# A planner entry for the expert products: a negative extra latency, priorities as before

## The chip, the cores and the metric

The kernel runs on one core of a Trainium2 chip. The metric is the device time of one execution in microseconds; of three runs shown for the kernel before the change the median is 987.2 us (985.83 to 988.81).

## What is computed

Three layers in one program: attention with rotary embedding, a dense feed-forward layer with a rational activation, and a mixture of experts with one expert per token. The change lies in the third.

```python
def _moe2_ref(x, w_gate, w1, w2):          # x: 2304 tokens x 512, 8 experts, hidden 1024
    logits = x @ w_gate
    expert_idx = np.argmax(logits, axis=1)
    ...
    for e in range(E):
        mask = expert_idx == e
        xe = x[mask]
        h = np.maximum(xe @ w1[e], 0.0)
        ye = h @ w2[e]
        out[mask] = gate_w[mask, None] * ye
```

## The kernel before

**The experts' tiles.** Tokens are sorted by expert into tiles t of at most 128 tokens. Every product is made of float32 values split into a high part (a rounded copy, made by ScalarE) and a low part (the value less its high part, made by VectorE or GpSimd), so one product is three matmuls: high by high, low by high, high by low. A tile has these steps, each an entry of a list with the name that the texts here use:

- `gx.t` (GpSimd, L925): an indirect DMA gathers the tile's rows. From t=10 on it takes its row numbers from a column that two small DMAs of SyncE bring in first, `cl.t` (L971).
- `xT.t` (TensorE, L1025): four transposes; `xH.et`, `xL.et` (ScalarE L1030, VectorE L1031): high and low part.
- `sA.t.c` (ScalarE, L1008) and `sL.t.c` (L1011; VectorE, but GpSimd for c=3 and c=7 and two others): high and low part of the weight piece c of the tile's expert, 128 by 1024. Pieces 0 to 3 belong to the first product, 4 to 7 to the second. A ring of five buffers holds the split pieces; `wl.t.c` (SyncE, L941) loads a raw piece once the low part of the tile before has been made from its buffer.
- `e1.t.k` (TensorE, L1044), k=0 to 3: the first product, six matmuls of 512 columns each, by weight piece k. Its last two read the low part `sL.t.k`.
- `rl.t` (ScalarE, L1050): the ReLU; `hT.t.0`, `hT.t.1` (TensorE, L1054): eight transposes; `hH.t.j`, `hL.t.j` (ScalarE L1060, VectorE L1061).
- `e2.t.k` (TensorE, L1071), k=0 to 3: the second product by weight piece 4+k, six matmuls; the third and the sixth read the low part.
- `fn.t` (L1077, L1078): scaling; `fs.t` (GpSimd, L1080): an indirect DMA scatters the rows to the output.

In the steady state TensorE does `e1` of tile t and then `e2` of tile t-1. While the first tiles run, VectorE also works through the second half of the routing, `B.c0` to `B.re` (L819 to L882), which places the remaining tokens; small copies for it run on ScalarE (L822, L824, L834, L844, L853, L854).

**What sets the order.** Nothing of this is written in the order in which it runs. `record` (L1113) and `step` (L1085) hand each step to `Plan.add` with an urgency, an engine, an assumed length `t`, what it reads and writes, and an extra latency `lat`. `Plan.order` (L85) then simulates five engines at build time: each takes, of the steps that are ready about now, the one with the lowest urgency. The instructions are emitted in that order, so it fixes the order on every engine. A step's result counts as ready at its end plus `AFTER` of its engine (0.3 us on TensorE) plus `lat`, and 0.1 us less for a step on the same engine:

```python
AFTER=dict(P=.3,V=.17,A=.17,G=.12,D=2.1)
...
x=end if ops[j][4]!=ops[i][4] or ops[i][4]=='D' else end-.1
if x>ready[j]: ready[j]=x
...
clock[e]=t+o[5]; end=t+o[5]+s.AFTER[e]+o[11]
```

Both products accumulate into one buffer (`eh`, `epsO`), so each `e1.t.k` depends on `e1.t.k-1`, and in this simulation it could start 0.2 us after that one's end at the earliest. The assumed times are used for the order alone; on the chip each instruction waits only for the semaphores of what it reads and writes.

Tiles 0 to 17 go through this list (`MIN`=18). What follows is emitted in a fixed order of code: `run` (L1134) and, here for the two last half tiles, `both` (L989).

Of the kernel before, what the change touches and what calls it, by code (L numbers as in the profile page):

```python
# [15 lines left out]
P=128  # L16
# [443 lines left out]
def phase1b(tc, plan, xT, w, ab, wg, x2, part, lg, ident, cp, xo3, keep, pre=()):  # L460
# [5 lines left out]
    if 1:  # L466
# [192 lines left out]
        for F in range(NS):  # L659
            s,k=steps[F]; h,g=ST[s]; t=TS(F); e=1 if last(F) else 0  # L660
            op(t+.1,f'm1.{F}',mm1,F)
            op(t+.8,f'au.{F}',a_u,F); op(t+.81,f'ae.{F}',a_e,F); op(t+.82,f'w1.{F}',a_w,F,0); op(t+.83,f'w2.{F}',a_w,F,1)
            op(t+2.2,f'p0.{F}',a_p,F,0); op(t+2.7,f'p1.{F}',a_p,F,1)
            t=TS(F+1)
            for d,n,fn,*a in ((.5,'ln',a_r,0),(.51,'ex',a_r,1),(.52,'q0',a_m,0),(.53,'q1',a_m,1),(1.5,'q2',a_m,2),(2.0,'gH',a_gH),(2.01,'gL',a_gL)): op(t+d,f'{n}.{F}',fn,F,*a)
            op(TS(F+LAG)+(0 if last(F) else .2),f'm2.{F}',mm2,F)
            if last(F):
                te=TS(F+LAG)
                for i in range(NTC): op(te+.4+.01*i,f'ev.{s}.{i}',o_ev,s,i); op(te+.405+.01*i,f'wr.{s}.{i}',o_wr,s,i)
                for i in range(NTC):  # L670
                    c=g*NTC+i
                    if h==0: continue
                    for d,x,n,fn in ((1,3.7,'tr',o_tr),(2,0,'sb',o_sb),(2,.1,'sl',o_sl)):
                        op(TS(F+LAG+d+i)+x if g<3 else TS(F+LAG+1)+1.4*i+.3*d+x/9 if g==3 else TS(F+LAG)+2+1.2*i+.3*d+x/9 if g==4 else te+.5+.9*i+.4*d+x/9,f'{n}.{c}',fn,c)
                if h:
                    for d,x,n,fn in ((NTC+1,3.7,'lg',o_lg),(NTC+2,0,'lc',o_lc),(NTC+2,3.7,'lt',o_lt),(NTC+3,0,'fi',o_fin)):
                        op(TS(F+LAG+d)+x if g<3 else TS(F+LAG+d-2)+x if g==3 else TS(F+LAG+d-3)+x if g==4 else te+3.2+.4*(d-NTC-1)+x/9,f'{n}.{g}',fn,g)
            if h==1 and k==len(FS[s])-4:
                t=max([t for n,t in rank.items() if n[:2]=='wr']+[TS(F)+3.5])
                for i in range(NTC): op(t+.01+.01*i,f'ld.{g*NTC+i}',o_ld,g*NTC+i)  # L680
# [214 lines left out]
class Experts:  # L895
# [147 lines left out]
            for hf in range(2):  # L1043
                s.T.matmul(h[hf],lhsT=d[z][:,k],rhs=w[wz][:,hf*512:hf*512+512],start=(k==0 and n==0),stop=(k==3 and n==2))  # L1044
    def mm1(s,t,k):
        s.op(f'e1.{t}.{k}',s.mm1_,t,k,eng='P',t=1.38,r=[(('eX',t%2),z) for z in 'HL']+[(('ew',t,k),z) for z in 'HL'],w=[(('eh',),0)],
            after=[f'{n}.{s.NS-1-i}' for n in ('ae','au','p0','p1') for i in range(2)] if t==k==0 else [])
    def relu_(s,t):
        d=s.D[t]; d['hr']=s.once(('hr',t%2),lambda: s.tag(6+t%2,1,2,512))
# [20 lines left out]
            for n,(z,wz) in enumerate((('hH',0),('hL',0),('hH',1))):  # L1070
                s.T.matmul(o,lhsT=d[z,j][:,kk],rhs=w[wz][:,i*512:i*512+512],start=(f==0 and n==0),stop=(f==7 and n==2))  # L1071
    def mm2(s,t,k):
        s.op(f'e2.{t}.{k}',s.mm2_,t,k,eng='P',t=1.38,r=[(('ehs',k//2,t%2),z) for z in 'HL']+[(('ew',t,4+k),z) for z in 'HL'],w=[(('epsO',),0)],after=['ev.11.2'] if t==k==0 else [])
    def fin_(s,t,z):
        g,i=s.rt.at(s.rt.gate,t); x,ix=s.rt.at(s.rt.sidx,t); o=s.once('o',lambda: s.tag(14,0,2,512))[:,t%2]
        if z==0:
            if t<4: s.A.activation(o,s.got['psO'],AF.Copy,scale=g[:,i:i+1])  # L1077
            else: s.V.tensor_scalar(o,s.got['psO'],g[:,i:i+1],None,ALU.mult)  # L1078
            return
        s.D.pop(t); s.nc.gpsimd.indirect_dma_start(out=s.out,out_offset=bass.IndirectOffsetOnAxis(ap=x[:,ix:ix+1],axis=0),in_=o,in_offset=None,bounds_check=NT-1,oob_is_err=False)  # L1080
# [100 lines left out]
```

## Time and profile before

| what | value |
|---|---|
| median of three runs | 987.2 us |
| the profiled execution's own time | 987.96 us |
| its span, first to last instruction | 986.2 us |
| TensorE busy | 946.6 us (96%) |
| VectorE, ScalarE, GpSimd busy | 826.9, 794.2, 746.5 us |
| mean granted TensorE clock | 0.993 |

The profiled execution is 0.8 us above the median, and 1.8 us of its time lie around its span. Its span has the attention first, the dense layer to about 738 us, an interleaved stretch in which the experts' first tiles and the routing run, and the experts alone from about 784 us on. PE is TensorE's matmuls, PEld its weight loads, DVE is VectorE, ACT ScalarE, POOL GpSimd, SPq the queue of SyncE, which issues DMAs. Matmuls are pipelined, so one of 512 columns is shown with some 0.4 us where its successor starts 0.23 us later.

### The profile page before, as it was taken

How to read it: one execution, taken by the hardware profiler on the slowest of the kernel's cores; microseconds unless marked ns; L12 is line 12 of the kernel's file. 1: busy time of each engine (PE TensorE's matmuls, PEld its weight loads, DVE VectorE, ACT ScalarE, POOL GpSimd, SP SyncE). 2: the span in 40 equal slices, each digit the busy share in tenths (PEclk: the TensorE clock that was granted, in tenths of full speed). 3: DMA queues.
4: the chain of work that ended last, by engine and by line, in shares of the span. 5: the costliest groups of instructions: out<-in, count | busy, mean ns of one | idle time of the engine just before them, and what ended most of it. 6: DMA issues, size and time to landing. Idle time of an engine off the chain costs nothing.

```text
span 986.2 us, 17395 instructions
## 1 busy us (share of the span) xinstructions
PE 946.6 (96%) x5402; PEld 834.4 (85%) x5402; DVE 826.9 (84%) x1451; ACT 794.2 (81%) x1538; POOL 746.5 (76%) x678
## 2 busy tenths in 40 slices
PE   5899999999988999999999999999999999999997
PEld 3889999999986898999999899898877788888873
DVE  6888999999999889999988676768998877777772
ACT  4899999999997888887777676766678788888881
POOL 3999999999448999998988576665574776767752
PEclk9999999999999999999999999999999999999999
DMA  7889797988724443432403021211611211561143
GB/s 241 236 226 220 208 226 209 228 209 194 207 84 153 142 137 121 137 122 78 146 2 96 11 87 28 80 40 34 231 53 49 49 40 54 180 227 44 44 123 106
DMA packets 55594, 125.81 MB, mean 128 GB/s; under 512 B 10947, under 2 KB 17219, under 8 KB 55492
## 3 DMA queue, kind: packets, MB, share of 16 engines
q1 hardware_dynamic: 52372, 114.65, 41.1%
q0 software_dynamic: 3120, 9.96, 3.2%
q8 instruction: 45, 0.74, 0.3%
q14 instruction: 57, 0.47, 0.2%
HBM read 146.63 MB, written 19.18 MB: 168 GB/s over the span
## 4 chain that ended last, share of the span: by engine, by line
PE 66%; ACT 12%; POOL 6%; DMA 6%; DVE 6%; issue 4%; SPq 0%; POOLq 0%; ACTq 0%; DVEq 0%
PE h L517 18%; PE acc L525 18%; PE h L1044 10%; PE acc L1071 9%; DMA st<-h 4%; ACT p L219 3%; ACT pTH L266 3%; PE sc L199 2%; PE ps L258 2%; PE av L280 2%; PE acc L1054 2%; ACT h L179 1%; POOL h L181 1%; ACT tm L286 1%; PE m L580 1%
## 5 line engine op out<-in xcount | busy, mean ns | idle before, releaser
L517 PE MATMUL h<-xH,w 128*128 128x384 f32 x768 | 214.3, 341 | 4.2 <-ACT gH L548 2.3
L525 PE MATMUL acc<-w,gH 128*128 128x512 f32 x576 | 150.0, 396 | 2.8 <-ACT gH L548 2.7
L517 PEld LDWEIGHTS h<-xH,w 128*128 128x128 f32 x768 | 140.9, 188 | 9.0 <-ACT gH L548 2.5
L517 PE MATMUL h<-xL,w 128*128 128x384 f32 x384 | 129.7, 338 | 0.0
L525 PEld LDWEIGHTS acc<-w,gH 128*128 128x128 f32 x576 | 107.5, 190 | 20.7 <-ACT gH L548 3.1
L199 PE MATMUL sc<-st 128*128 128x288 f32 x512 | 97.4, 314 | 14.6 <-DVE st L315 10.1
L551 POOL TENSOR_TENSOR gL<-e,gH 128x384 fp32r<-128x384 f32 x96 | 98.3, 1024 | 17.3 <-ACT gH L548 15.9
L532 POOL TENSOR_SCALAR w<-u,bb 128x384 f32<-128x384 f32 x96 | 65.3, 680 | 60.8 <-ACT u L528 53.8
L268 DVE TENSOR_TENSOR pTL<-ps,pTH 128x512 fp32r<-128x512 f32 x144 | 98.6, 686 | 15.0 <-ACT pTH L266 12.0
L212 DVE TENSOR_REDUCE nm<-sc 128x1 f32<-128x576 f32 x144 | 106.3, 748 | 4.9 <-PE sc L199 3.3
L533 POOL TENSOR_TENSOR w<-u,w 128x384 f32<-128x384 f32 x96 | 97.7, 1018 | 7.3
L219 ACT ACTIVATE p<-sc,nm 128x576 f32<-128x576 f32 x128 | 95.6, 747 | 2.7 <-DVE nm L212 2.3
L199 PEld LDWEIGHTS sc<-st 128*128 128x128 f32 x512 | 75.4, 194 | 20.1 <-DVE st L315 10.9
L266 ACT ACTIVATE pTH<-ps 128x512 fp32r<-128x512 f32 x144 | 86.4, 602 | 5.5 <-PE ps L258 3.9
L540 ACT ACTIVATE r<-w,c 128x384 f32<-128x384 f32 x96 | 59.1, 615 | 38.8 <-POOL w L533 37.7
L544 DVE SCALAR_TENSOR_TENSOR w<-w,y 128x384 f32<-128x384 f32 x96 | 53.0, 552 | 44.3 <-ACT y L541 41.5
L1011 POOL TENSOR_TENSOR ew<-w,ew 128x1024 fp32r<-128x1024 f32 x22 | 63.7, 2894 | 34.3 <-ACT ew L1008 34.2
L525 PE MATMUL acc<-w,gL 128*128 128x512 f32 x288 | 82.4, 394 | 0.0
L258 PE MATMUL ps<-ident,p 128*128 128x128 f32 x512 | 80.3, 281 | 0.3 <-DVE pTL L268 0.3
L280 PE MATMUL av<-pTH,vv 128*128 128x256 f32 (+1 forms) x256 | 79.6, 326 | 0.6 <-DVE R L255 0.4
L517 PEld LDWEIGHTS h<-xL,w 128*128 128x128 f32 x384 | 72.4, 188 | 2.4
L280 PE MATMUL av<-pTL,vv 128*128 128x256 f32 (+1 forms) x256 | 71.9, 296 | 1.7 <-DVE pTL L268 1.7
(297 smaller groups left out, 2686.2 us busy)
## 6 DMA issues: line engine op xcount, KB each, us to landing
w<-wl SPq DMA_DIRECT2D x102, 512.0 KB
raw<-wl SPq DMA_DIRECT2D x60, 512.0 KB
raw<-wio SPq DMA_DIRECT2D x32, 512.0 KB
st<-h SPq DMA_DIRECT2D x30, 432.0 KB
x<-kq SPq DMA_DIRECT2D x17, 576.0 KB
xr<-xT SPq DMA_DIRECT2D x48, 192.0 KB
st<-h SPq DMA_DIRECT2D x30, 288.0 KB
w<-kq SPq DMA_DIRECT2D x13, 576.0 KB
```

The lines of the kernel that those rows point to most:

```text
L199: T.matmul(sc[:,hf,:288],lhsT=fl[j][:,q0:q0+128],rhs=S[j][:,2*kk,hf*288:hf*288+288],start=(kk==0),stop=(kk==1))
L212: V.tensor_reduce(d['nm'],d['sc'][:,:,:288],AX.XY,ALU.max,negate=True)
L219: A.activation(pv.rearrange('p (a b)->p a b',a=2),d['sc'][:,:,:288],AF.Exp,bias=d['nm'],accum_out=w['su'][:,i:i+1])
L258: for kc in range(4): T.transpose(d['ps'][:,kc],d['p'][:,o+kc*128:o+kc*128+128],ident)
L266: A.activation(d['Hd'],d['src'],AF.Copy)
L268: d=U[u]['D'][i]; V.tensor_tensor(d['Ld'],d['src'],d['Hd'].bitcast(F32),ALU.subtract)
L280: T.matmul(av,lhsT=w['vv'][:,4*j+kc,:],rhs=w[z,hf][:,kc,320*j:320*j+N],start=(kc==0 and z=='H'),stop=False)
L517: T.matmul(h,lhsT=W[f,0][:,wz,kd*128:kd*128+128],rhs=d[xz][:,kd],start=(n==0),stop=(n==11)); n+=1
L525: T.matmul(acc[s][c],lhsT=d[z][:,c*128:c*128+128],rhs=W[f,1][:,wz],start=(k==0 and n==0),stop=(last(F) and n==2))
L533: else: G.tensor_tensor(d['w'],d['u'],d['w'],ALU.mult)
L551: G.tensor_tensor(d['gL'],d['e'],d['gH'].bitcast(F32),ALU.subtract)
L1044: s.T.matmul(h[hf],lhsT=d[z][:,k],rhs=w[wz][:,hf*512:hf*512+512],start=(k==0 and n==0),stop=(k==3 and n==2))
```

## The change

The two lines that enter the experts' products into the list get `lat=-.2`, so that in the planner's simulation a product's part is ready for its successor on TensorE at once, and for other engines 0.1 us after its end rather than 0.3. Urgencies, lengths and dependencies stay.

```diff
     def mm1(s,t,k):
-        s.op(f'e1.{t}.{k}',s.mm1_,t,k,eng='P',t=1.38,r=[(('eX',t%2),z) ...
+        s.op(f'e1.{t}.{k}',s.mm1_,t,k,eng='P',t=1.38,lat=-.2,r=[(('eX',t%2),z) ...
...
     def mm2(s,t,k):
-        s.op(f'e2.{t}.{k}',s.mm2_,t,k,eng='P',t=1.38,r=[(('ehs',k//2,t%2),z) ...
+        s.op(f'e2.{t}.{k}',s.mm2_,t,k,eng='P',t=1.38,lat=-.2,r=[(('ehs',k//2,t%2),z) ...
```

No instruction is added or removed. On each engine some change places. On TensorE this is so at three places only, around tiles 9, 13 and 17; on VectorE `hL.t.1` comes ahead of `sL.t.4` in most tiles from 4 on; on SyncE the columns `cl.t` and some loads trade places with a neighbour; on GpSimd a gather passes a weight piece three times.

**First place: ScalarE, between tiles 1 and 2, where the second half of the routing begins** (`w_0_10014` is the output of `fn.0`, `m` the routing's bank, `ew_9519<-w_0_9397` is `sA.1.4`, and `w_1` written from `acc` are `hH.1.0` and `hH.1.1`; in brackets what a row waits for). Before:

```order
L582 ACTIVATE x2T<-m_9988 32x384 [waits PE_49]
L1077 ACTIVATE w_0_10014<-acc_9946,r_gtA 128x512 [waits PE_49]
L822 ACTIVATE m_10026<-r_b 128x8 [waits DVE_49,Activation_49]
L824 ACTIVATE m_10026<-m_10026 128x48 [waits DVE_49,Activation_49]
L1060 ACTIVATE w_1_9902<-acc_9884 128x512 [waits PE_49]
L1008 ACTIVATE ew_9519<-w_0_9397 128x1024 [waits DMAHW7_49,Pool_49]
L1060 ACTIVATE w_1_9916<-acc_9891 128x512 [waits PE_49]
```

Now:

```order
L582 ACTIVATE x2T<-m_9988 32x384 [waits PE_49]
L1077 ACTIVATE w_0_10014<-acc_9947,r_gtA 128x512 [waits PE_49]
L1008 ACTIVATE ew_9519<-w_0_9397 128x1024 [waits DMAHW7_49,Pool_49]
L822 ACTIVATE m_10027<-r_b 128x8 [waits DVE_49,Activation_49]
L824 ACTIVATE m_10027<-m_10027 128x48 [waits DVE_49,Activation_49]
L1060 ACTIVATE w_1_9902<-acc_9884 128x512 [waits PE_49]
L1060 ACTIVATE w_1_9916<-acc_9892 128x512 [waits PE_49]
```

`sA.1.4` moved up by three rows, ahead of the routing's two small copies. VectorE's list is the same here in both; it begins the routing's second half as follows, and its L822 waits for the ScalarE copy of L822 (the Activation semaphore), its L825 for that of L824:

```order
L587 TENSOR_TENSOR lg<-m_7500,lg 128x24 [waits DVE_49]
L822 TENSOR_REDUCE m_10027<-lg 128x6 [waits DVE_49,Activation_49]
L823 TENSOR_TENSOR m_10027<-lg,m_10027 128x48 [waits DVE_49]
L825 TENSOR_TENSOR m_10027<-lg,m_10027 128x48 [waits Activation_49]
L826 TENSOR_TENSOR m_10027<-m_10027,r_cnt 128x48 [waits DVE_49]
```

**Second place: TensorE after the first product of tile 9** (L1025 is `xT.10`, L1054 is `hT.9`, the rows of L1071 ahead belong to `e2.8.1`, those behind to `e2.8.2`). Before:

```order
L1071 MATMUL acc_9946<-w_0_9718,w_1_9903 128x512
L1071 MATMUL acc_9946<-w_0_9719,w_1_9902 128x512
L1025 MATMUL y<-ident,xL 128x128 x4
L1071 MATMUL acc_9946<-w_0_9728,w_1_9916 128x512
L1071 MATMUL acc_9946<-w_0_9728,w_1_9917 128x512
```

Now:

```order
L1071 MATMUL acc_9947<-w_0_9718,w_1_9903 128x512
L1071 MATMUL acc_9947<-w_0_9719,w_1_9902 128x512
L1025 MATMUL y<-ident,xL 128x128 x4
L1054 MATMUL acc_9884<-ident,w_1_9954 128x128 x4
L1054 MATMUL acc_9892<-ident,w_1_9954 128x128 x4
L1071 MATMUL acc_9947<-w_0_9728,w_1_9916 128x512
L1071 MATMUL acc_9947<-w_0_9728,w_1_9917 128x512
```

The eight transposes `hT.9` moved up from behind `e2.8.3` to ahead of `e2.8.2`; likewise `xT.11` moved up in the next tile, from behind `e2.9.1` to behind `e1.10.1`. With them VectorE's list of this tile became `xL.e10`, `hL.9.0`, `fn.8`, `hL.9.1`, `sL.10.2`, `sL.9.4`, `sL.9.5`, `sL.9.6`, `xL.e11`; before it was `xL.e10`, `sL.10.2`, `fn.8`, `hL.9.0`, `sL.9.4`, `hL.9.1`, `sL.9.5`, `sL.9.6`. Tiles 13 and 14 repeat this, and at tile 17 `hT.17` passes `e2.16.2` and `e2.16.3`.

**Third place: GpSimd in tile 8** (L1080 is `fs.6`, the L1011 with `ew_9520` is `sL.7.7`, L925 is the gather `gx.11`). Before:

```order
L1011 TENSOR_TENSOR w_0_9719<-w_0_7536,w_0_9718 128x1024 [waits DMAHW4_49,PE_49,Activation_49]
L1080 DMA out<-w_0_10014,r_TB 2304x512 [waits DMASW7_49,DVE_49]
L1011 TENSOR_TENSOR ew_9520<-w_0_9420,ew_9520 128x1024 [waits DMAHW2_49,PE_49,Activation_49]
L925 DMA w_0_9742<-x_71,r_WA 128x512 [waits DMAHW2_49,DMAHW1_49,DMASW3_49]
L1011 TENSOR_TENSOR ew_9519<-w_0_7536,ew_9519 128x1024 [waits DMAHW7_49,PE_49,Activation_49]
```

Now:

```order
L1011 TENSOR_TENSOR w_0_9719<-w_0_7536,w_0_9718 128x1024 [waits DMAHW4_49,PE_49,Activation_49]
L1080 DMA out<-w_0_10014,r_TB 2304x512 [waits DMASW7_49,DVE_49]
L925 DMA w_0_9742<-x_71,r_WA 128x512 [waits DMAHW1_49,DMAHW0_49,DMASW3_49]
L1011 TENSOR_TENSOR ew_9520<-w_0_9420,ew_9520 128x1024 [waits DMAHW2_49,PE_49,Activation_49]
L1011 TENSOR_TENSOR ew_9519<-w_0_7536,ew_9519 128x1024 [waits DMAHW7_49,PE_49,Activation_49]
```

The gather, which waits for the two DMAs of its column, now stands ahead of the low part of a weight piece. `gx.15` and `gx.19` do the same in tiles 12 and 16. On SyncE `cl.11` was issued behind `wl.9.3` and `wl.8.4`; now it follows `wl.9.3`.

## Rows read from the trace of the kernel before

**Rows 1.** TensorE's and the others' busy time by stage (start:end, length, busy us)

```profile
core 0: us, PE busy (x) PEld busy (x) DVE busy (x) ACT busy (x) POOL busy (x), PEclk, DMA share, GB/s
738.50:770.40 31.90, 29.02 (x153) 23.44 (x151) 26.79 (x61) 26.22 (x41) 17.02 (x7) 1.00 0.12 42
770.40:952.80 182.40, 182.40 (x884) 150.23 (x885) 144.63 (x156) 154.31 (x189) 133.74 (x60) 1.00 0.33 102
952.80:986.20 33.40, 27.14 (x129) 14.35 (x127) 13.29 (x12) 11.20 (x16) 6.97 (x5) 0.96 0.26 83
```

**Rows 2.** Timeline of TensorE, 762 to 771 us (start, length, idle before and its releaser)

```profile
764.70 1.20 PE L1071 MATMUL acc<-ew,w 128*128 128x512 f32 x4 [1.62 <-DVE ew L1011]
...
770.38 0.73 PE L1044 MATMUL h<-ew,xL 128*128 128x512 f32 x2 [1.26 <-DVE xL L1031]
```

**Rows 3.** Timeline of ScalarE, 752 to 756 us

```profile
752.81 0.69 ACT L1077 ACTIVATE w<-acc,r_gtA 128x512 f32<-128x512 f32 x1 [0.91 <-PE acc L1071]
753.40 0.17 ACT L822 ACTIVATE m<-r_b 128x8 f32<-128x8 f32 x1
754.17 0.20 ACT L824 ACTIVATE m<-m 128x48 f32<-128x48 f32 x1 [0.60 <-DVE m L823]
...
754.75 1.07 ACT L1008 ACTIVATE ew<-w 128x1024 fp32r<-128x1024 f32 x1
```

**Rows 4.** Timeline of VectorE, 753 to 764 us

```profile
753.62 0.21 DVE L822 TENSOR_REDUCE m<-lg 128x6 f32<-128x48 f32 x1
...
755.26 0.68 DVE L1061 TENSOR_TENSOR w<-acc,w 128x512 fp32r<-128x512 f32 x1
...
760.38 0.21 DVE L845 TENSOR_TENSOR r_r<-m,r_cum 128x48 f32<-128x48 f32 x1 [0.24 <-ACT r_ntB L844]
...
762.91 0.32 DVE L861 SCALAR_TENSOR_TENSOR m<-m,r_r 128x144 f32<-128x144 f32 x1 [0.39 <-ACT r_WA L854]
...
763.43 1.22 DVE L1011 TENSOR_TENSOR ew<-w,ew 128x1024 fp32r<-128x1024 f32 x1
```

**Rows 5.** Timeline of TensorE in tiles 9 and 10

```profile
855.05 0.60 PE L1025 MATMUL y<-ident,xL 128*128 128x128 f32 x4
...
864.71 2.95 PE L1071 MATMUL acc<-ew,w 128*128 128x512 f32 x12
867.50 0.60 PE L1025 MATMUL y<-ident,w 128*128 128x128 f32 x4
867.85 1.64 PE L1071 MATMUL acc<-ew,w 128*128 128x512 f32 x6
```

**Rows 6.** Timeline of ScalarE after the first product of tile 9

```profile
852.23 1.09 ACT L1050 ACTIVATE w<-h 128x512 f32<-128x512 f32 x2 [0.52 <-PE h L1044]
```

**Rows 7.** Timeline of GpSimd in tiles 8 to 10

```profile
839.33 2.85 POOL L1011 TENSOR_TENSOR ew<-w,ew 128x1024 fp32r<-128x1024 f32 x1 [1.41 <-ACT ew L1008]
842.32 1.85 POOL L925 DMA_INDIRECT w<-x,r_WA  x1
...
858.00 2.84 POOL L1011 TENSOR_TENSOR w<-w,w 128x1024 fp32r<-128x1024 f32 x1 [1.38 <-ACT w L1008]
...
864.24 2.82 POOL L1011 TENSOR_TENSOR w<-w,w 128x1024 fp32r<-128x1024 f32 x1 [1.44 <-ACT w L1008]
868.93 1.26 POOL L925 DMA_INDIRECT xL<-x,r_WA  x1 [1.87 <-DMA r_WA<-td]
```

**Rows 8.** Timeline of GpSimd and VectorE, 732 to 738 us: two subtractions that overlap

```profile
732.72 3.39 POOL L1011 TENSOR_TENSOR ew<-w,ew 128x1024 fp32r<-128x1024 f32 x1
...
733.76 3.43 DVE L1011 TENSOR_TENSOR ew<-raw,ew 128x1024 fp32r<-128x1024 f32 x1
```

**Rows 9.** Timeline of SyncE's queue in tiles 8 and 10

```profile
835.97 1.29 SPq L941 DMA_DIRECT2D w<-wl  x2
838.27 1.37 SPq L971 DMA_DIRECT2D r_WA<-td  x2
...
862.77 1.24 SPq L971 DMA_DIRECT2D r_WA<-td  x2
```

**Rows 10.** SyncE's load of a column's expert number (L930), 937 to 942 us

```profile
L930 SPq TENSOR_LOAD <-r_WA x1: 273/273/273, 940.3 to 940.3; - x1
```

**Rows 11.** SyncE's queue, 937 us, the column of that load

```profile
937.87 1.42 SPq L971 DMA_DIRECT2D r_WA<-td  x2
```

**Rows 12.** Chain of waits in order of time, second product of tile 7

```profile
843.15 2.80 PE acc L1071 x12
```

More of the change, by code (lines that the diff above doesn't have):

```diff
@@ L1045, in mm1 @@
     def mm1(s,t,k):
-        s.op(f'e1.{t}.{k}',s.mm1_,t,k,eng='P',t=1.38,r=[(('eX',t%2),z) for z in 'HL']+[(('ew',t,k),z) for z in 'HL'],w=[(('eh',),0)],
+        s.op(f'e1.{t}.{k}',s.mm1_,t,k,eng='P',t=1.38,lat=-.2,r=[(('eX',t%2),z) for z in 'HL']+[(('ew',t,k),z) for z in 'HL'],w=[(('eh',),0)],
             after=[f'{n}.{s.NS-1-i}' for n in ('ae','au','p0','p1') for i in range(2)] if t==k==0 else [])
@@ L1072, in mm2 @@
     def mm2(s,t,k):
-        s.op(f'e2.{t}.{k}',s.mm2_,t,k,eng='P',t=1.38,r=[(('ehs',k//2,t%2),z) for z in 'HL']+[(('ew',t,4+k),z) for z in 'HL'],w=[(('epsO',),0)],after=['ev.11.2'] if t==k==0 else [])
+        s.op(f'e2.{t}.{k}',s.mm2_,t,k,eng='P',t=1.38,lat=-.2,r=[(('ehs',k//2,t%2),z) for z in 'HL']+[(('ew',t,4+k),z) for z in 'HL'],w=[(('epsO',),0)],after=['ev.11.2'] if t==k==0 else [])
     def fin_(s,t,z):
```

## The prediction

> **What bounds the kernel now.** I read the stages first. From 770.4 to 952.8 us, which is tiles 3 to 17, TensorE is busy for 182.40 of 182.40 us at a granted clock of 1.00, which is the 2.4 GHz level [rows 1]. The reader is to see that nothing is to be won there by another order: the same matmuls in another sequence take as long, and an earlier `hT` or `xT` can only fill a hole that is not there. What a new order can do there is make TensorE wait. In the last 33.4 us TensorE is idle for 33.40 - 27.14 = 6.3 us, and from 738.5 to 770.4 for 31.90 - 29.02 = 2.9 us [rows 1]. Next the waits of TensorE in that earlier stretch: the two large ones, 1.62 and 1.26 us, both end when VectorE has finished something, `sL.1.5` at L1011 and `xL.e3` at L1031 [rows 2]. So the chain that sets the end runs through VectorE up to 770.4 us and through TensorE from there on, and whatever shifts VectorE ahead of 764 us shifts the end.
>
> Third, VectorE and ScalarE at that spot. VectorE begins the routing's second half at 753.62 and reaches `sL.1.5` at 763.43 [rows 4]. In between it is idle for 0.24 and 0.39 us for ScalarE's small copies [rows 4], which themselves wait for VectorE, so these holes move with it and absorb nothing.
>
> **The change, step by step.**
>
> *`sA.1.4` ahead of the routing's copies (first place).* VectorE's L822 began at 753.62, just after ScalarE's copy of L822 had ended at 753.40 + 0.17 = 753.57 [rows 3, 4]; the list says that it waits for that copy. Now `sA.1.4` stands ahead of the copy. It takes 1.07 us, and ScalarE starts the next operation about 0.1 us ahead of the end of one (752.81 + 0.69 = 753.50 against 753.40) [rows 3], so the copy comes 0.97 us later, at 754.37, and VectorE's L822 at 754.59. The next pair, L823 to ScalarE's L824, only follows: ScalarE had waited 0.60 us for it [rows 3] and will wait again. `hL.1.0`, which began at 755.26 [rows 4], follows the routing's first steps in VectorE's list and begins at 756.23; `sL.1.5` moves from 763.43 to 764.40. TensorE's wait at 764.70 then ends at 765.67, and the one at 770.38, whose producer stands further down the same list, at 771.35. From there on TensorE has no hole that could take it up [rows 1]. **Term: +0.97 us.** Below, the price is 0 if VectorE should not have waited for that copy or caught up; above, 1.07 us, the whole length of `sA.1.4`. I take 0.97, since both ends of the hand-over are in the rows.
>
> *`hT.9` ahead of `e2.8.2` (second place; also tiles 13 and 17).* It needs the ReLU, which ended at 852.23 + 1.09 = 853.32 [rows 6]; `hT.9` now follows `xT.10`, which starts at 855.05 and takes 0.35 us of TensorE (867.50 to 867.85 for the same four transposes) [rows 5]. At 855.40 the ReLU is 2.1 us old. Cost 0, gain 0, as TensorE has no hole here.
>
> *What this drags along on VectorE and GpSimd (tiles 10 and 14).* The moved transposes make `e2.8.2` and `e2.8.3` some 0.8 us later, and with them `sA.10.3` and GpSimd's `sL.10.3`, which ran from 858.00 for 2.84 us [rows 7] and now ends about 861.6. VectorE has `sL.10.2` behind `hL.9.1` and meets it. How two such subtractions meet is shown by one pair: VectorE's, begun at 733.76, took 3.43 us rather than 1.22 [rows 4, 8], and ended 1.08 us after GpSimd's had ended at 732.72 + 3.39 = 736.11. So `sL.10.2` ends about 861.6 + 1.1 = 862.7. TensorE reads it in the fifth matmul of `e1.10.2`. Twelve matmuls take 867.50 - 864.71 = 2.79 us [rows 5], 0.23 each; `e1.10.2` begins 12 matmuls ahead of 864.71 and, with `xT.11` now in front of it, 0.35 later, at 862.27, and reads the low part at 863.2. It has 0.5 us to spare. Then `sL.9.4` and `sL.9.5` follow to about 865.0; GpSimd's `sL.9.7`, begun at 864.24 [rows 7], comes 0.35 us later and holds VectorE's `sL.9.6` until about 867.3, so this ends at 868.4. TensorE reads it in the third matmul of `e2.9.2`, at 867.85 + 0.46 = 868.3 [rows 5]. That is a tie: 0 in the sum, 0 to 0.5 us in each of the two tiles for the range.
>
> The Trainium skill, "SBUF — State Buffer", section "Who interferes with whom", states this as an exclusive lock: a VectorE instruction with two SBUF inputs and a GpSimd one that reads SBUF block each other, and the one that issues first keeps the ports for its whole length. The pair above agrees. By that rule the tie goes against this change whenever `sL.9.7` issues first; a rule of shared bandwidth would stretch both a little and leave the tie open.
>
> *`gx.11` ahead of `sL.7.7` (third place; also `gx.15`, `gx.19`).* The gather waits for its column. Behind `wl.9.3`, issued at 835.97, the column's first DMA can go 1.0 us later (838.27 less the end of the pair of loads, 837.26), its second some 0.9 us after that, as the pair took 1.37 us and one of them is estimated at half a us of issue: at 837.9 [rows 9]. How long a column takes to land the trace shows only by bounds: below 2.4 us, since SyncE's load of such a column ran at 940.3 after an issue at 937.87 [rows 10, 11]; and once, from a last issue ending at 862.77 + 1.24 = 864.01, 4.9 us until the gather that waited for it began at 868.93 [rows 7, 9]. With 2.4 us the gather begins at 840.3 and ends 1.85 us later, at 842.2; `sL.7.7`, which ran from 839.33 for 2.85 us, ends at 845.0 [rows 7]. TensorE reads it in the third matmul of `e2.7.3`, at 843.15 + 1.40 + 0.46 = 845.0 [rows 12]. I take 0: 2.4 us is a bound and not the length, and rows 10 and 11 are of a stretch like these. With 4.9 us it would be 2.5 us of waiting at that tile.
>
> *`hL.t.1` ahead of `sL.t.4` (most tiles from 4 on), the order of SyncE's loads, the end.* 0.68 us of VectorE pass ahead of a piece that TensorE needs only after the next `e1`, twice the 2.79 us of twelve matmuls, or 5.6 us [rows 5]; loads go out at most a us earlier or later, a whole tile ahead of their use. At the end `hT.17` passes two products, and the products then follow: 0.
>
> **Sum.** 987.96 + 0.97 = 988.9 us for an execution like the profiled one, which is 0.8 us above the median shown; against that median, 987.2 + 1.0 = **988.2 us**.
>
> **Rivals.**
> 1. *The delay is not passed on*: VectorE's L822 is held by something else, or the two waits of TensorE have another last releaser. For it: GpSimd and ScalarE steps stand in the same stretch. Against it: 0.05 us between the copy's end and L822, and VectorE's list without other holes. 987.2 us.
> 2. *The ports decide against VectorE*: about 0.5 us in tiles 10 and 14 each and 0.2 us at each of the three gathers. For it: the tie above. Against it: TensorE's every wait gives VectorE the same time back. 987.2 + 1.0 + 1.6 = 989.8 us.
> 3. *The gather blocks GpSimd* (this one ends slower): a column lands after 4.9 us rather than 2.4, and the low part behind the gather is late by 2.5 us. It decides from 2.4 us on, us for us. For it: the one gather that is seen to wait, and loads under way in tile 8. Against it: that wait fell into the stretch with the densest loads, the others had none. In two of three tiles: 988.2 + 5.0 = 993.2 us.
> 4. *The end gets shorter*: with `hT.17` done earlier its high parts come earlier and some of the 6.3 us in which TensorE is idle at the end go. For it: these holes. Against it: two products of 1.4 us trade places with transposes of 0.8, and half the holes lie behind the last matmul. At most half of 6.3: 988.2 - 3.1 = 985.1 us.
>
> **How the numbers follow.** Chances: forecast 0.60, first rival 0.10, second 0.17, third 0.08, fourth 0.05. About 0.3% (3.0 us) is what a measurement can tell from no change. The forecast and the first two rivals lie within 984.2 to 990.2; of the second and the scatter I give 0.05 to slower, which with the third makes 0.13. Only the fourth can be faster, and with scatter 0.04. That leaves 0.83. The runs shown lie 1.4 below and 1.6 us above their median; from the first rival's 987.2 less 1.4 to the second's with a little less than its scatter the range is 985.8 to 990.8, with the third and fourth left out.
>
> **What would show it.** In the changed kernel's profile ScalarE's L822 should come behind an L1008, VectorE's L822 about 1.0 us later after `lg`, TensorE's waits for L1011 and L1031 near 765.7 and 771.3 grow to 2.6 us and stay, and 770 to 954 us should have no wait of TensorE. Waits of L1071 for VectorE in tile 9's second product, or for GpSimd in tile 7's, 11's or 15's, would make rivals 2 and 3 right; a shorter last stretch rival 4. The forecast is wrong if TensorE waits at all between 772 and 953 us for more than 2 us, or if the first term is missing.

## The result and the profile after

| | before | the change |
|---|---|---|
| median of ten runs, us | 988.1 (985.7 to 989.3) | 992.6 (990.0 to 997.1) |
| ratio, with its 95% interval | | 1.0052 (1.0041 to 1.0064) |
| the profiled execution's own time and span, us | 987.96, 986.2 | 991.22, 989.4 |
| start of the first ReLU of tile 1 in it | 744.78 | 745.14 |
| from there to the end of the span | 241.4 | 244.3 |

The changed kernel is slower by half a per cent, some 5 us, and its runs lie further apart. The forecast of 988.2 us and its range up to 990.8 us were wrong; only the third rival, with a chance of 0.08, ended there (993.2 us). Of the 4.4 us between the forecast and 992.6 us, 0.9 us is the base: over ten runs the kernel before has 988.1 us, where the three runs shown had 987.2. The last line of the table is used below for all kernels: nothing that differs begins before tile 1, and the start of tile 1 alone varies by up to 3.4 us between the executions below (742.69 to 746.09 us). By it the profiled execution of the change lost 2.8 us, less than the 4.5 us between the medians; executions that lost more are read in the experiments 5 and 6.

The first term came as forecast. ScalarE around the routing's copies, start and length, then idle time and its releaser:

```profile
753.21 0.69 ACT L1077 ACTIVATE w<-acc,r_gtA 128x512 f32<-128x512 f32 x1 [0.91 <-PE acc L1071]
753.79 1.05 ACT L1008 ACTIVATE ew<-w 128x1024 fp32r<-128x1024 f32 x1
754.74 0.17 ACT L822 ACTIVATE m<-r_b 128x8 f32<-128x8 f32 x1
```

and VectorE, which now waits for that copy:

```profile
753.73 0.18 DVE L587 TENSOR_TENSOR lg<-m,lg 128x24 f32<-128x24 f32 x1
754.95 0.21 DVE L822 TENSOR_REDUCE m<-lg 128x6 f32<-128x48 f32 x1 [1.04 <-ACT m L822]
```

`sA.1.4` stands ahead of the copy, VectorE idles 1.04 us where it had idled hardly at all [rows 3, 4]. The waits of TensorE that the view names from there to the end (the second row is none, it shows the twelve matmuls behind the first):

```profile
766.03 1.20 PE L1071 MATMUL acc<-ew,w 128*128 128x512 f32 x4 [2.21 <-DVE ew L1011]
767.07 2.93 PE L1071 MATMUL acc<-w,w 128*128 128x512 f32 x12
...
771.71 0.74 PE L1044 MATMUL h<-ew,xL 128*128 128x512 f32 x2 [1.25 <-DVE xL L1031]
...
846.68 1.21 PE L1071 MATMUL acc<-ew,w 128*128 128x512 f32 x4 [0.34 <-POOL ew L1011]
...
956.82 1.20 PE L1071 MATMUL acc<-ew,w 128*128 128x512 f32 x4 [1.03 <-DVE ew L1011]
```

The first of [rows 2] has become 2.21 us, the second has kept its length, and two are new: one for GpSimd's `sL.7.7` in tile 8, one for VectorE's `sL.16.5` at the end. By the starts of the ReLUs the loss of 2.84 us (244.26 less 241.42) is 0.96 up to tile 3, 0.60 between the tiles 3 and 11, and 1.3 in the last stretch. The stages that answer to [rows 1]:

```profile
738.86:771.71 32.85, 29.32 (x153) 23.38 (x151) 26.79 (x61) 26.21 (x41) 16.99 (x7) 1.00 0.12 41
771.71:954.69 182.98, 182.64 (x884) 150.21 (x885) 154.47 (x155) 154.46 (x189) 126.77 (x60) 1.00 0.32 98
954.69:989.40 34.71, 27.39 (x129) 14.22 (x127) 16.25 (x14) 11.20 (x16) 6.56 (x5) 0.95 0.30 99
```

In the middle stage VectorE was busy for 144.63 us with 156 instructions; now it is busy for 154.47 us with 155. GpSimd went the other way, from 133.74 to 126.77 us. No instruction was added: VectorE's are longer because they are held up. That alone is not the loss: experiment 3 below loses nothing, and VectorE is busy there for 150.53 us of the same stage.

```profile
770.05:952.40 182.35, 182.35 (x884) 150.36 (x885) 150.53 (x156) 154.57 (x189) 128.85 (x60) 1.00 0.33 101
```

What counts is where VectorE is held. Tile 8 shows it, and by whom. GpSimd there in the changed kernel:

```profile
837.34 1.02 POOL L1080 DMA_INDIRECT out<-w,r_TB  x1 [0.16 <-issue]
843.11 1.04 POOL L925 DMA_INDIRECT w<-x,r_WA  x1 [4.76 <-PE acc L1071]
844.19 2.44 POOL L1011 TENSOR_TENSOR ew<-w,ew 128x1024 fp32r<-128x1024 f32 x1
846.82 3.15 POOL L1011 TENSOR_TENSOR ew<-w,ew 128x1024 fp32r<-128x1024 f32 x1 [0.19 <-ACT ew L1008]
```

Its column on SyncE's queue, both DMAs and then the second alone:

```profile
837.95 1.62 SPq L971 DMA_DIRECT2D r_WA<-td  x2
...
839.06 0.51 SPq L971 DMA_DIRECT2D r_WA<-td  x1
```

And VectorE, before:

```profile
841.81 2.58 DVE L1011 TENSOR_TENSOR w<-raw,w 128x1024 fp32r<-128x1024 f32 x2 [1.91 <-ACT w L1008]
```

and now:

```profile
843.13 4.58 DVE L1011 TENSOR_TENSOR w<-raw,w 128x1024 fp32r<-128x1024 f32 x2 [2.16 <-ACT w L1008]
847.64 0.68 DVE L1031 TENSOR_TENSOR xL<-y,xH 128x512 fp32r<-128x512 f32 x1
```

GpSimd idles for 4.76 us ahead of `gx.11`. The view names TensorE as the releaser, which had long been done; the column is what came last, 843.11 - (837.95 + 1.62) = 3.5 us after its second DMA had been issued; experiment 4, which moves the column alone, takes this wait away. So `sL.7.7`, which ran from 839.33 before [rows 7], runs from 844.19. That is just where VectorE does its pair `sL.9.0`, `sL.9.1`: 2.58 us before, 4.58 now. In the old order the gather lay beside this pair [rows 7] and did it no harm.

At the end it is the same with one more step. GpSimd around `gx.19`:

```profile
942.15 1.04 POOL L925 DMA_INDIRECT xL<-x,r_WA  x1 [3.61 <-PE h L1044]
943.21 2.41 POOL L1011 TENSOR_TENSOR ew<-w,ew 128x1024 fp32r<-128x1024 f32 x1
...
953.29 2.40 POOL L1011 TENSOR_TENSOR w<-w,w 128x1024 fp32r<-128x1024 f32 x1 [1.21 <-ACT w L1008]
```

VectorE's `sL.17.0` before, and VectorE beside these rows now:

```profile
941.47 1.38 DVE L1011 TENSOR_TENSOR ew<-raw,ew 128x1024 fp32r<-128x1024 f32 x1 [1.96 <-ACT ew L1008]
```

```profile
943.35 3.36 DVE L1011 TENSOR_TENSOR ew<-raw,ew 128x1024 fp32r<-128x1024 f32 x1 [2.18 <-ACT ew L1008]
...
953.45 3.32 DVE L1011 TENSOR_TENSOR ew<-w,ew 128x1024 fp32r<-128x1024 f32 x1
956.69 1.21 DVE L1011 TENSOR_TENSOR w<-w,w 128x1024 fp32r<-128x1024 f32 x1
```

The late `sL.15.7` gets in at 943.21, 0.14 us ahead of VectorE's `sL.17.0`, and costs it 2.1 us (3.36 against 1.2 undisturbed). VectorE is late at 953.45, again 0.16 us behind GpSimd, pays 2.1 us a second time, and TensorE waits 1.03 us.

### The profile page after: what moved, and what is told of

Its sections match the earlier page's. It is cut to its first block, busy times and chain, and to the rows that moved or that the text cites. A ratio compares the mean times of both kernels' runs of the same rounds, so it can differ in the third digit from the quotient of the medians.

```text
span 989.4 us, 17391 instructions
## 1 busy us (share of the span) xinstructions
PE 948.3 (96%) x5402; PEld 836.2 (85%) x5402; DVE 839.6 (85%) x1451; ACT 793.8 (80%) x1538; POOL 738.5 (75%) x678
## 4 chain that ended last, share of the span: by engine, by line
PE 65%; ACT 13%; DVE 6%; POOL 6%; DMA 5%; issue 4%; SPq 0%; POOLq 0%; ACTq 0%; DVEq 0%
PE h L517 18%; PE acc L525 18%; PE h L1044 9%; PE acc L1071 9%; ACT p L219 4%; ACT pTH L266 3%; DMA st<-h 3%; PE sc L199 2%; PE av L280 2%; PE ps L258 2%; PE acc L1054 2%; ACT tm L286 1%; ACT h L179 1%; POOL h L181 1%; DVE ew L1011 1%
## 5 line engine op out<-in xcount | busy, mean ns | idle before, releaser
L1011 POOL TENSOR_TENSOR ew<-w,ew 128x1024 fp32r<-128x1024 f32 x22 | 63.2, 2875 | 32.1 <-ACT ew L1008 32.0
```

## The experiments

Theory from this profile: **the gathers**. The three gathers hold GpSimd while their columns are under way; the late low parts then meet VectorE's subtractions, and TensorE waits for VectorE. With `sA.1.4`'s 0.97 us that would be the whole loss of this execution. Rival: **the ports alone**, that is VectorE's new order around tiles 9, 13 and 17 meets GpSimd's subtractions, gathers or not. A further idea came with the results: that chance decides part of it, and that TensorE's clock does.

All variants keep the planner's list and move single steps in it afterwards:

```diff
-        return [ops[i] for _,_,i in res]
+        return moved(dep,ops,[ops[i] for _,_,i in res])
```

where `moved` takes each step of a list MOVE out and puts it right behind or ahead of another. Only the MOVE lines are shown below. The results, one row per kernel, each against the kernel before run beside it; the last column is the profiled execution's span less the start of the first ReLU of tile 1 (before: 241.4, the change: 244.3).

| kernel | ratio to before, 95% interval | from tile 1 to the end, us |
|---|---|---|
| 1 gathers back | 1.0036 (1.0021 to 1.0050) | 988.7 - 742.69 = 246.0 |
| 2 gathers only | 1.0057 (1.0039 to 1.0074) | 993.6 - 746.09 = 247.5 |
| 3 gathers and `sA.1.4` back | 1.0008 (0.9994 to 1.0023) | 986.1 - 744.45 = 241.7 |
| 4 columns early | 1.0023 (1.0011 to 1.0035) | 988.6 - 746.04 = 242.6 |
| 5 the change again | 1.0042 (1.0027 to 1.0057) | 992.2 - 743.78 = 248.4 |
| 6 the change, third | one run, 999.9 us | 998.0 - 745.09 = 252.9 |
| 7 `sA.1.4` only | 1.0013 (1.0001 to 1.0026) | 987.1 - 743.31 = 243.8 |
| 8 a longer hole | 1.0034 (1.0019 to 1.0049) | 988.1 - 744.21 = 243.9 |
| 9 VectorE first | 1.0010 (0.9999 to 1.0021) | 986.6 - 744.95 = 241.7 |
| 10 VectorE first, second form | 1.0027 (1.0014 to 1.0040) | 988.9 - 743.88 = 245.0 |
| 11 one wait | 1.0006 (0.9997 to 1.0015) | 988.1 - 745.50 = 242.6 |
| 12 mended | 1.0004 (0.9995 to 1.0013) | 985.6 - 743.95 = 241.7 |

### 1. The change with the three gathers put back

```diff
+MOVE=[('gx.11','behind','sL.7.7'),('gx.15','behind','sL.11.7'),('gx.19','behind','sL.15.7')]
```

> The changed kernel with gx.11, gx.15 and gx.19 put back behind sL.7.7, sL.11.7 and sL.15.7 on GpSimd; all else as changed. Gather theory (the three gathers hold GpSimd while their columns are under way, and the late low parts cost the rest): ratio to the kernel before 1.001, only ScalarE's 0.97 us is left; no wait of TensorE near 846.7 and 956.8 us, and a scatter like that of before. Port theory (VectorE's new order around tiles 9, 13 and 17 meets GpSimd's subtractions): ratio 1.004, the wait near 956.8 stays.

Neither theory came out whole. The ratio, 1.0036, is the port theory's 1.004 and not the gather theory's 1.001; but the waits near 846.7 and 956.8 us are gone, which was the gather theory's sign, and the execution has others (1.15 us at 817.65 and 1.10 us at 893.74, both for VectorE's L1011). What is left of the change beside the gathers costs more than 0.97 us here. Experiment 3 shows that it takes `sA.1.4` for that, and experiment 7 how it can go.

### 2. Before, with the three gathers alone moved ahead

```diff
+MOVE=[('gx.11','ahead','sL.7.7'),('gx.15','ahead','sL.11.7'),('gx.19','ahead','sL.15.7'),
+      ('cl.11','behind','wl.9.3'),('cl.15','behind','wl.13.3'),('cl.19','behind','wl.17.3')]
```

> The kernel before with only the three gathers moved ahead of sL.7.7, sL.11.7 and sL.15.7 and their columns' DMAs one load earlier, as in the change; TensorE, VectorE and ScalarE keep the order of before. Gather theory: ratio 1.003 to 1.004, GpSimd idle for 3 us or more ahead of the three gathers. Port theory: ratio 1.000 to 1.001, since VectorE's order is the old one.

The gathers alone are enough, and dearer than I had put them: TensorE, VectorE and ScalarE keep their old order, and yet 6.1 us are lost (247.5 against 241.4). GpSimd idles 4.49, 2.70 and 3.03 us ahead of the three. The port theory, which needs VectorE's new order, is not needed for a loss of this size. TensorE's new waits in this execution:

```profile
847.78 1.20 PE L1071 MATMUL acc<-ew,w 128*128 128x512 f32 x4 [1.43 <-POOL ew L1011]
...
954.02 0.74 PE L1044 MATMUL h<-ew,xL 128*128 128x512 f32 x2 [2.48 <-DVE xL L1031]
```

with a third between them, 1.15 us at 908.22 for VectorE. One is the wait for the low part itself; the larger one comes by way of VectorE.

### 3. The change with the gathers and `sA.1.4` put back

```diff
+MOVE=[('gx.11','behind','sL.7.7'),('gx.15','behind','sL.11.7'),('gx.19','behind','sL.15.7'),
+      ('sA.1.4','behind','hH.1.0')]
```

> The changed kernel with the three gathers put back and sA.1.4 put back behind the routing's copies on ScalarE; what is left of the change is the order around tiles 9, 13 and 17, hL.t.1 ahead of sL.t.4, and SyncE's loads. Gather theory with ScalarE's term: ratio 0.999 to 1.001. Port theory: ratio 1.003.

As the gather theory said, and the port theory's 1.003 lies outside the interval. What is left, the order around tiles 9, 13 and 17, `hL.t.1` ahead of `sL.t.4` and SyncE's loads, costs nothing that is seen by itself: 0.2 us from tile 1 on, no new wait of TensorE over 0.25 us. Against experiment 1, where `sA.1.4` alone stands otherwise, that is 0.28% less.

### 4. The change with the columns issued earlier

```diff
+MOVE=[('cl.11','ahead','wl.9.0'),('cl.15','ahead','wl.13.0'),('cl.19','ahead','wl.17.0')]
```

> The changed kernel with only SyncE's order altered: the columns cl.11, cl.15 and cl.19 are issued ahead of the four loads that stood ahead of them, some 5 us earlier. Gather theory in its narrow form (what costs is the wait for the column, not the place of the gather): GpSimd no longer idles ahead of the three gathers, ratio 1.001 to 1.002. Wide form (a gather in that place is dear even with its column there, as it shifts the low part into VectorE's subtractions): ratio 1.003 to 1.005.

The profile decides for the narrow form; the ratio, 1.0023, lies just above that form's range, and its interval reaches into the wide one's. The gathers stand where the change put them, GpSimd idles 0.3 us ahead of each, and none of the waits of tile 8 or of the end is there. GpSimd in tile 8:

```profile
839.55 2.09 POOL L925 DMA_INDIRECT w<-x,r_WA  x1 [0.30 <-issue]
841.67 2.47 POOL L1011 TENSOR_TENSOR ew<-w,ew 128x1024 fp32r<-128x1024 f32 x1
```

and VectorE:

```profile
844.03 2.36 DVE L1011 TENSOR_TENSOR w<-raw,w 128x1024 fp32r<-128x1024 f32 x2 [2.16 <-ACT w L1008]
```

The low part is done at 844.1, and VectorE's pair, begun at 844.03, takes 2.36 us. The execution loses 242.56 - 241.42 = 1.1 us from tile 1 on, and by the ReLU of tile 3 it has lost 0.9 of it: `sA.1.4`.

### 5 and 6. The change again, twice

No edit.

> The changed kernel once more, for a second profiled execution. Gather theory: GpSimd idles 3 to 5 us ahead of gx.11, gx.15 and gx.19 in every execution, so the idle of 4.76, 2.96 and 3.61 us comes back within 1 us; TensorE's waits that follow may differ in place; ratio 1.004 to 1.006. Lottery theory (which of VectorE and GpSimd gets its subtraction in first is decided by tens of ns, and the loss differs from execution to execution): waits of TensorE for L1011 at other places than 846.7 and 956.8 us, times 4 us or more apart.

> The changed kernel a third time, one look. Gather theory: idle of GpSimd of about 4.5, 3 and 3.5 us ahead of the three gathers again. Lottery theory: the stretch from the ReLU of tile 1 to the end, 244.3 and 248.4 us in the two executions so far, is another value between 243 and 249.

Both theories hold: GpSimd's idle time ahead of the gathers comes back each time (4.29, 3.05 and 3.54 us in the second execution, 4.46, 2.70 and 3.54 in the third), but what it costs does not. The second lost 7.0 us from tile 1 on, the third 11.5, more than I had thought possible. In the second, tile 8 alone loses some 4 us. GpSimd:

```profile
841.28 1.04 POOL L925 DMA_INDIRECT w<-x,r_WA  x1 [4.29 <-PE acc L1071]
842.35 2.41 POOL L1011 TENSOR_TENSOR ew<-w,ew 128x1024 fp32r<-128x1024 f32 x1
845.46 2.62 POOL L1011 TENSOR_TENSOR ew<-w,ew 128x1024 fp32r<-128x1024 f32 x1 [0.71 <-ACT ew L1008]
```

VectorE:

```profile
841.77 7.39 DVE L1011 TENSOR_TENSOR w<-raw,w 128x1024 fp32r<-128x1024 f32 x2 [2.17 <-ACT w L1008]
849.09 0.68 DVE L1031 TENSOR_TENSOR xL<-y,xH 128x512 fp32r<-128x512 f32 x1
```

TensorE:

```profile
849.82 1.22 PE L1044 MATMUL h<-w,xL 128*128 128x512 f32 x2 [2.49 <-DVE xL L1031]
850.84 1.91 PE L1044 MATMUL h<-w,xH 128*128 128x512 f32 x4
```

and the stages there (columns as in [rows 1]):

```profile
846.00:849.80 3.80, 1.33 (x10) 0.90 (x8) 3.80 (x3) 1.89 (x3) 2.08 (x1) 0.95 0.00 0
849.80:852.50 2.70, 2.68 (x6) 2.16 (x7) 2.70 (x4) 1.06 (x1) 1.74 (x1) 0.50 0.52 117
```

Two subtractions of VectorE take 7.39 us instead of 2.58: the second ends at 849.16, 1.08 us after GpSimd's second one at 848.08. `xL.e9` behind them is late, TensorE has a hole of 2.49 us, and after it the granted clock is 0.50, the 1.2 GHz level: four matmuls take 1.91 us where four take 1.09 to 1.10 in undisturbed stretches. So this place costs more than its wait. In the third execution the hole in front of `xL.e13` was 2.39 us, and the clock fell there too.

### 7. Before, with `sA.1.4` alone moved ahead

```diff
+MOVE=[('sA.1.4','ahead','B.bk')]
```

> The kernel before with only sA.1.4 moved ahead of the routing's two copies on ScalarE; the other engines keep their order. My sum: VectorE's L822 1.0 us later behind L587, TensorE's wait for sL.1.5 2.2 us rather than 1.6 and what follows 0.97 us later to the end, ratio 1.001. Lottery theory: 0.97 us in most executions, and in some 1 to 4 us more by subtractions of VectorE that GpSimd holds up, ratio 1.002 to 1.003 and a wider scatter.

Ratio 1.0013, an interval that holds my sum and the larger number, but the profile speaks for chance. The hole is 2.20 us as it should be. TensorE behind it, and the stage:

```profile
764.17 1.67 PE L1071 MATMUL acc<-ew,w 128*128 128x512 f32 x4 [2.20 <-DVE ew L1011]
765.65 4.07 PE L1071 MATMUL acc<-w,w 128*128 128x512 f32 x12
...
792.67 1.19 PE L1071 MATMUL acc<-w,w 128*128 128x512 f32 x4 [1.05 <-DVE w L1011]
```

```profile
764.00:768.00 4.00, 3.83 (x10) 3.01 (x11) 3.73 (x11) 1.81 (x3) 2.36 (x1) 0.59 0.00 0
```

The same twelve matmuls took 2.93 us at a clock of 1.00 in the change's first profile. With the four ahead of them they are 1.6 us longer (769.72 - 764.17 = 5.55 us against 770.00 - 766.03 = 3.97). That is taken up almost at once, since TensorE need not wait for `xL.e3` any more: the ReLU of tile 3 is 1.03 us late instead of 0.96. But ScalarE's next high part (begun at 768.07) waits for these matmuls and GpSimd's low part for that, and VectorE pays:

```profile
769.21 2.41 POOL L1011 TENSOR_TENSOR w<-w,w 128x1024 fp32r<-128x1024 f32 x1 [2.85 <-ACT w L1008]
```

```profile
770.15 2.54 DVE L1011 TENSOR_TENSOR ew<-raw,ew 128x1024 fp32r<-128x1024 f32 x1
```

This subtraction took 1.34 us in the kernel before. VectorE loses 1.2 us, meets GpSimd again in the tiles 3 and 4, and TensorE waits 1.05 us at 792.67. Experiment 1's execution went the same way: the clock lowered behind the same hole, and the other waits later. So the 0.97 us of `sA.1.4` are the least that it costs. Of the six profiled executions with this hole, the three in which the clock fell behind it have a further wait of over 1 us between the ReLUs of the tiles 4 and 7, and the other three have none. Experiment 8, with another list, had the lower clock and no such wait, so a lower clock is not enough by itself.

### 8. Before, with a longer hole

```diff
+MOVE=[('B.pl1','ahead','sL.1.5'),('B.sl','ahead','sL.1.5')]
```

> The kernel before with one step moved on VectorE: sL.1.5 goes behind the routing's B.pl1 and B.sl, 2.05 us later; all else keeps its order. TensorE's wait of 1.62 us for it becomes some 3.7 us. Clock theory (a hole of 2.2 us, as sA.1.4 makes it, is at the edge at which the granted clock falls to 0.50 for about 3 us; a longer one falls each time): the windows behind the hole show 0.50, twelve matmuls take 4 us and more instead of 2.91, and some of it is taken up by the wait of 1.26 us that follows; ratio 1.001 to 1.003. Rival (the two lowered clocks had another cause): clock 1.00 behind the hole, ratio 1.000 to 1.001.

The hole became 4.28 us rather than 3.7, and the clock fell, with the wait of 1.26 us gone as expected; the twelve matmuls took 3.40 us and not 4:

```profile
766.79 2.08 PE L1071 MATMUL acc<-ew,w 128*128 128x512 f32 x4 [4.28 <-DVE ew L1011]
768.66 3.40 PE L1071 MATMUL acc<-w,w 128*128 128x512 f32 x12
```

```profile
766.70:769.50 2.80, 2.71 (x6) 2.15 (x7) 2.77 (x5) 0.98 (x1) 0.00 (x0) 0.50 0.00 0
```

The ratio, 1.0034, lies a little above the range for the clock theory and well above the rival's. That a longer hole makes the clock fall each time is not so: it stayed at 1.00 behind a hole of 2.48 us in experiment 2 and one of 2.47 us in experiment 6.

### 9, 10 and 11. Towards a version that beats both

Both large waits of the kernel before are for VectorE, so moving the awaited steps up in VectorE's list should gain 1.2 to 2.9 us.

```diff
+MOVE=[('sL.1.5','ahead','B.c3'),('B.bt0','behind','rl.2'),('sL.3.0','ahead','B.pl1'),('xL.e3','ahead','B.oh2')]
```

> The kernel before with four places changed in VectorE's list where the routing's second half runs: sL.1.5 ahead of B.c3, sL.3.0 ahead of B.pl1, xL.e3 ahead of B.oh2, and B.bt0 behind rl.2 (so that the ReLU does not wait for its copy). If VectorE's list is what holds TensorE for 1.62 and 1.26 us there, both waits go and the end comes 2 to 2.9 us earlier, ratio 0.997 to 0.998. If GpSimd's or ScalarE's steps are late next, the waits come back within 10 us, ratio 0.999 to 1.001.

```diff
+MOVE=[('sL.1.5','ahead','B.c3'),('B.bt0','behind','rl.2'),('sL.3.0','ahead','B.pl1'),('xL.e3','ahead','B.pl1'),('sL.2.5','ahead','hL.2.1')]
```

> The kernel before with VectorE's list changed as in the earlier trial, and two places more: xL.e3 behind sL.3.0 (it was ahead of B.oh2), and sL.2.5 ahead of hL.2.1 so that it issues ahead of GpSimd's sL.2.7. If both of TensorE's waits go and VectorE is not held by GpSimd in tiles 3 and 4: the stretch from the ReLU of tile 1 to the end is 238.7 to 239.5 us instead of 241.4, ratio 0.997 to 0.998. If VectorE is held again: a wait of TensorE of about 1 us near tile 4, ratio 0.999 to 1.000.

```diff
+MOVE=[('xL.e3','ahead','B.oh2'),('sL.2.5','ahead','hL.2.1')]
```

> The kernel before with two steps moved on VectorE: xL.e3 ahead of B.oh2, and sL.2.5 ahead of hL.2.1. TensorE's wait of 1.62 us stays, the one of 1.26 us should go. If the rest follows TensorE: the stretch from the ReLU of tile 1 to the end is 240.2 us instead of 241.4, ratio 0.998 to 0.999. If VectorE, which is not earlier itself, is held by GpSimd in tiles 3 and 4 as in the first trial: a wait of 1 us there gives it back, ratio 0.999 to 1.001.

None gained, and the second form was slower. In the first, the ReLU of tile 3 came 1.3 us earlier, counted from that of tile 1, and the gain was gone by tile 5. The third shows why most plainly; its waits for `sL.1.5` and `xL.e3` are 1.61 us and none, and then GpSimd and VectorE meet:

```profile
784.78 2.42 POOL L1011 TENSOR_TENSOR ew<-w,ew 128x1024 fp32r<-128x1024 f32 x1
```

```profile
784.41 3.88 DVE L1011 TENSOR_TENSOR ew<-raw,ew 128x1024 fp32r<-128x1024 f32 x1
```

VectorE itself is no earlier than before, only TensorE is; VectorE is held here and again at 790.55, and TensorE waits 1.07 us behind the ReLU of tile 4. In the second form a hole of 1.90 us in tile 3 was followed by the lower clock for some ten microseconds, the longest seen:

```profile
774.00:780.00 6.00, 6.00 (x20) 5.03 (x20) 5.18 (x9) 2.03 (x3) 2.91 (x2) 0.50 0.00 0
```

A version that beats the kernel before was not found.

### 12. The change with both causes taken away

```diff
+MOVE=[('cl.11','ahead','wl.9.0'),('cl.15','ahead','wl.13.0'),('cl.19','ahead','wl.17.0'),('sA.1.4','behind','hH.1.0')]
```

> The changed kernel with the two suspected causes taken away and all else as changed: the columns are issued some 5 us earlier on SyncE (the gathers stay ahead of their low parts), and sA.1.4 is back behind the routing's copies. If these two are the whole cause: ratio 0.999 to 1.001, and 241.4 to 241.9 us from the ReLU of tile 1 to the end. If the order around tiles 9, 13 and 17 costs something by itself: ratio 1.002 or more.

1.0004, and 241.65 us from tile 1 on, as in experiment 3. Within the interval the two causes are the whole loss: the columns' late landing and `sA.1.4`'s place. They have no fixed prices that add up. Three pairs of kernels differ in `sA.1.4`'s place alone, and by their ratios it costs 1.3 us (experiment 7 and before), 1.9 us (4 and 12) and 2.8 us (1 and 3), each known to about 1.5 us. The late columns cost 1.9 to 2.9 us in the change where the columns are issued earlier (its ratios 1.0052 and 1.0042 against 1.0023 in experiment 4), 0.6 to 1.6 us where the gathers are put back (1.0036 in experiment 1), and 5.6 us without the rest of the change (experiment 2).

## Why the prediction was wrong

**What bounds the kernel** was read rightly: VectorE up to tile 3, TensorE from there, and whatever makes TensorE wait there is lost.

**`sA.1.4`**: the hand-over behind the term of +0.97 us was right. VectorE's L822 idled 1.04 us for the copy, and tile 3's ReLU came 0.96 us later. Of its signs, the two waits did not grow to 2.6 us: the first grew to 2.21 us and the second kept its length, since the matmuls ahead of them came later too; the ends moved as forecast. As a price over many executions the term looks too small: 1.3 to 2.8 us, each known to about 1.5 us (experiment 12). Left out was that the hole of 1.62 us, now 2.2 us, is followed by the lower clock in some executions: in three of the six profiled ones that have this hole, and in none of the five that have the hole of 1.6 us.

**`hT.9` ahead of `e2.8.2` and what it drags along**: cost 0, as taken. The tie foreseen at the third matmul of `e2.9.2` did not become a wait (experiments 3 and 12).

**`gx.11` ahead of `sL.7.7`**: this is the step that failed, where the prediction says "I take 0"; in the first profile the waits behind the late columns lost 0.60 us in tile 8 and 1.3 us at the end, and in experiment 2, with the gathers alone moved, 6.1 us were lost. Three things were wrong in it.
- The landing of a column. The bound of 2.4 us was the load of one number of the column, which the first of its two DMAs brings [rows 10, 11]; the gather needs both. The time of the issue was right: 839.06 us for the second DMA, less the 0.36 us by which tile 1 was late in this execution and the 0.96 us of the first term, is 837.7 against 837.9. But from there to the gather it took 843.11 - 839.06 = 4.05 us instead of 2.4. From the end of the second issue it was 3.5 us in tile 8, 2.1 us in tile 12 (issued by 889.57, gather at 891.70) and 2.2 us in tile 16 (by 939.94, at 942.15); over the four executions with late columns it was 3.1 to 4.1 us in tile 8 and 2.1 to 2.7 us in the other two. Loads were under way in tile 8, as the third rival says (the DMA engines were busy for 0.52 of these 3.5 us, and for 0.23 and 0.03 in the other two tiles); that they cause the difference is not shown. The Trainium skill, "DMA: Bandwidth & Descriptors", section "Anatomy of one DMA — SWDGE (gpsimd) path", puts a fixed cost of about 2 us on a DMA that GpSimd issues, most of it for the confirmation that the last byte has landed. The columns go by SyncE's queue instead; two of the three rows lie near that figure, the one of tile 8 does not.
- Who waits for it. The working asked only whether TensorE would need `sL.7.7` before it is there, and found a tie. The wait was 0.34 us, but by two errors that nearly cancel: the landing 1.65 us longer, and gather and subtraction 1.04 and 2.44 us long instead of 1.85 and 2.85, which makes 1.2 us less. It did not ask what GpSimd's subtraction would meet 5 us later than before. The gather used to lie beside VectorE's pair `sL.9.0`, `sL.9.1` and to cost it nothing; the subtraction in its place cost the pair 2.0 us in the first profile (4.58 against 2.58) and 4.8 us in experiment 5 (7.39).
- The second rival had the meeting of the two engines, but at 0.2 us for each gather and mainly in tiles 10 and 14, where it did no harm.

**The end**: taken as 0, measured 1.3 us, by `gx.19` and the held `sL.16.5`.

**The third rival** gave nearly the measured time by luck, for a mechanism that is only half of it: the low part's own lateness cost TensorE 0.34 us in the profiled execution and 1.43 us in experiment 2, against the 2.5 us priced per tile. The larger part came through VectorE and the clock.

**The sign of being wrong**, waits of more than 2 us between 772 and 953 us, does not show in the first profile, which has 0.34 us there; it shows in the second and third (2.49 us at 849.82, and 2.47 and 2.39 us).

On the meeting itself, the subtractions of VectorE held above end 1.08 us or a little more behind GpSimd's end, as 953.45 + 3.32 = 956.77 against 953.29 + 2.40 = 955.69, which is nearly one undisturbed length of 1.2 us. The Trainium skill, "SBUF — State Buffer", section "Who interferes with whom", has VectorE and GpSimd block each other for whole instructions, and the rows agree. By the same section the order of issue decides who is blocked, and there the rows seem to differ: VectorE's row at 841.77 in experiment 5 began ahead of GpSimd's subtraction at 842.35 and was held nevertheless (see the last section).

What stays open: the share of the loss that each of the three gathers has on average, since it differed between executions; whether the new order around the tiles 9, 13 and 17 adds to what `sA.1.4` costs, as experiment 1 beside 7 may suggest; and what decides whether the clock falls after a hole of about 2 us.

## What to carry to other kernels

A step that waits for a DMA is priced not by what it delivers but by everything queued behind it on its engine, and by what that work will meet when it runs later; in a steady state in which two engines fit between each other's instructions, as here, a shift of a few us is not free just because nothing on the critical engine reads it soon. Before pricing such a wait, look for a row of exactly that transfer (here two DMAs, not one). And a hole in TensorE's work is worth its length only as long as the clock stays up.

## What was not expected of the hardware

- **The granted clock fell behind holes of some 2 us, but not each time.** From tile 1 on, holes of TensorE of 1.0 to 1.7 us were never followed by a lower clock in these profiles. Of twelve holes of 1.9 to 4.3 us seven were: three of the six of 2.2 us in the routing, the ones of 2.49 us (experiment 5), 2.39 us (6), 4.28 us (8) and 1.90 us (10), while holes of 2.48 us (2) and 2.47 us (6) were not. The lower stretch lasted some 3 us, once some ten.
- **A lead of 0.14 us went with a loss of 2 us.** GpSimd's `sL.15.7` began 0.14 us ahead of VectorE's `sL.17.0` and the latter took 3.36 us instead of 1.38 (at 941.47 in the kernel before). With the same instructions in the same order the stretch from tile 1 on was 244.3, 248.4 and 252.9 us in three executions. That such small leads make this difference is argued, not shown.
- **Meetings can go on without a cost.** From tile 1 on the kernel before has one VectorE subtraction of more than 1.6 us. In the experiments 7, 9 and 11 there are 30 or 31: from tile 5 on one is held to 1.8 to 2.0 us twice in every tile, nearly to the end, and TensorE waits for none of them.
- **Beginning first does not always keep a subtraction from being held.** VectorE's row at 841.77 in experiment 5 began 0.58 us ahead of GpSimd's subtraction at 842.35, while the gather ahead of that was still running (to 842.32), and it was held through it; so was the one at 784.41 in experiment 11, beside a gather that ran to 784.77. In experiment 7 a VectorE subtraction at 871.24, 0.39 us ahead of a gather's end and with GpSimd's subtraction at 871.66, took its undisturbed 1.21 us. What tells these apart was not found.
